# Attention's value loads put two groups ahead into the weights' raw buffers, and zero matmuls in the gaps before the gather

## The chip, the core and the metric

The kernel runs on one core of a Trainium2 chip, as one program in one launch. The metric is the device time of that launch in microseconds (us). Before the change its median is 881.94 us over three runs, 879.71 to 887.55.

## The reference

Three layers run one after the other, all in float32:

- attention over q, k, v of shape 4 x 12 x 448 x 64, with a sigmoid in place of the softmax: `sigmoid(q k^T / 8 - log 448) v`. Its output is the matrix x of 1792 tokens by 768;
- a mixture of 8 experts in which every expert takes exactly 224 tokens. The 1792 x 8 logits `x @ w_gate` are walked from the largest down; a pair (token, expert) is taken where the token is still free and the expert not yet full. Each expert then computes `relu(x @ w1[e]) @ w2[e]` on its tokens;
- a dense layer on the result: `h = x @ w_in`, `g = s * relu(h)^2 + b`, `g @ w_out`.

## The kernel before, in words

The order of the work is written out by hand: each engine runs its instructions in the order in which the Python code names them, and semaphores do the rest. All loads of the first stages are issued by one queue, SP, in order; a load whose buffer is not free holds back everything behind it. SP's transfers carry eight completion counters in turn, so a transfer also waits until the one eight places ahead has landed.

**Attention** runs over 12 groups `q` (three to each of the 4 batches). A group is two pairs `2q` and `2q+1` of two heads. Its values are one tile `vt` (128 x 7 x 128: three blocks of 128 keys for each pair, and in the middle the last 64 keys of both), loaded by `load_v` into two buffers. A pair's q and k are one tile `rqk`, loaded by `load_qk` in two transfers into five buffers. Each group has two halves, and in each half the code names:

- `split_qk`, on DVE: `rqk` of a pair of group q+2 is cut into a high part `wh` (L282) and a rest `wl` (L283);
- `values(q, half)`, on PE: the sigmoid weights times `vt` (L334, and L328 for the last 64 keys);
- every third group, for the batch before: `gate` and `gate_turn` (L354, L366);
- `scores(q+1, ...)`, on PE: three matmul terms of `wh` and `wl` for each block of keys (L310), each followed by a sigmoid on ACT;
- `convert`, on DVE (three times in group 4, else once or twice a group): w_in and w_out come as 64-bit floats and are made 32-bit in five DVE steps (four for later ones), from `craw` (768 KB a load, `cv_in`) to `co`, which goes back to memory as `nw` (`cv_out`). A `craw` load waits for the third of those steps (L155).

At the start of group q SP is given `load_qk` for the pairs 2q+5 and 2q+6 and `load_v` for group q+1. In the last two groups the first four experts' weights are loaded too (`w_dma`, five buffers `raw` of 128 x 768).

**The auction** then finds the assignment in eight steps (`auction`), a chain of small operations that hands from DVE to PE to DVE. In its gaps PE transposes x to rows (L508), ACT copies them out and SP stores them to `xs`. `keep_clock` (L418) multiplies zeros into a bank of PSUM that nobody reads.

**The places**: `settle` and `places` turn the choice into a list of row numbers `idx`: a running count (L612 to L618), 16 one-hot tiles `oh` on DVE (L626), 32 matmuls with them on PE (L634), two sums on DVE (L638). POOL then gathers the first expert's rows `xr` (L648). While that runs, PE is given `WARM[1]` zero matmuls; all engines then read a flag that decides the branch into more auction steps. PE goes on with 12 transposes of `xr` (L748) and the first expert's matmuls (L757 with `wh`, L758 with `wl`). From here to the end PE has work nearly all the time.

Of the kernel before, what the change touches and what calls it, by code (L numbers as in the profile page):

```python
# [8 lines left out]
F32 = mybir.dt.float32  # L9
# [10 lines left out]
B, H, S, D = 4, 12, 448, 64  # L20
# [4 lines left out]
CP = 112  # L25
NC = S // CP
NCH = NT // CP
# [9 lines left out]
STEPS = 8  # L37
MORE = (3, 8)
AHEAD = (2, 3, 4, 5, 6)
WARM = (7, 10, 2, 3)  # L40
ROWS = (3, 3, 3, 2, 2, 2, 2, 2)
SYNC = 0
SIGNS = 2
# [3 lines left out]
NQ = B * NP // 2  # L47
# [15 lines left out]


@with_exitstack
def tile_kernel(ctx, tc, qT, kT, v, wg, w1, w2, wi, wo, s2, b2, cst, out):
    nc = tc.nc
    V, A, G, T = nc.vector, nc.scalar, nc.gpsimd, nc.tensor

# [50 lines left out]
    cgp = early.enter_context(tc.tile_pool(name="cgp", bufs=1))  # L120

    att = ExitStack()
    qk = att.enter_context(tc.tile_pool(name="qk", bufs=5))
    vp = att.enter_context(tc.tile_pool(name="vp", bufs=2))
    at = att.enter_context(tc.tile_pool(name="at", bufs=2))
    ps_s = att.enter_context(tc.tile_pool(name="ps_s", bufs=3, space=PSUM))
# [9 lines left out]
    def cv_in():  # L136
        if todo:
            i = todo.pop(0)
            src, k, n = wide[i]
            craw[i] = cgp.tile([128, 768, 2], I32, name="craw", bufs=3)  # L140
            nc.sync.dma_start(craw[i].rearrange("p a b -> p (a b)"), src[n].bitcast(I32).rearrange("p k c -> p (k c)"))
            coming.append(i)
# [117 lines left out]
        nu["use"] += 1  # L260
        return splits.pop(i)

    raw_qk, two_qk, vt, attn, pvs, plg, lgs, pts = {}, {}, {}, {}, {}, {}, {}, {}
    pairs = [(b, p) for b in range(B) for p in range(NP)]

    def load_v(q):
        vt[q] = vp.tile([128, 7, 128], F32, name="vt", bufs=2)
        nc.sync.dma_start(vt[q], v[q // 3, q % 3])

    def load_qk(i):  # L270
        b, p = pairs[i]
        r = qk.tile([128, 2, S], F32, name="rqk")
        nc.sync.dma_start(r[:, 1], kT[b, p])
        nc.sync.dma_start(r[:, 0], qT[b, p])
        raw_qk[i] = r
# [42 lines left out]
                    two_qk.pop(n)  # L318

    def values(q, block):  # L320
        v = vt[q]
        pvs[q, block] = pv = ps_v.tile([128, 512], F32, name="pv")
        if block:
            a = attn.pop((q, 3))
            for n in range(2):
                rows = slice(n * 64, n * 64 + 64)
                for j in range(2):
                    T.matmul(pvs[q, n][j * 64:(j + 1) * 64, :S], v[rows, 3, j * D:(j + 1) * D], a[rows, j],  # L328
                             start=(n == 1), stop=(n == 0), skip_group_check=True)
            done(q, 0)  # L330
        for c in range(3):
            a = attn.pop((q, 4 * block + c))
            for j in range(2):
                T.matmul(pv[j * 64:(j + 1) * 64, :S], v[:, 4 * block + c, j * D:(j + 1) * D], a[:, j],  # L334
                         start=(block == 0 and c == 0), stop=(block == 1 and c == 2), skip_group_check=True)
        if block:
            done(q, 1)
# [75 lines left out]
    zero = ep.tile([128, 512], BF16, name="zero")  # L413
    V.memset(zero, 0.0)

    def keep_clock(n, p):
        for _ in range(n):
            T.matmul(p, zero[:, :CP], zero, start=True, stop=True)  # L418

    keep_clock(WARM[0], small_psum()[:CP])  # L420
    warm = ep.tile([1, 1], F32, name="warm")
# [8 lines left out]
    load_qk(2)  # L430
    load_qk(3)
    cv_in()
    cv_in()
    cv_in()
    scores(0, range(7))
    load_qk(4)
    nc.sync.dma_start(sb2[:, 0:1], s2.partition_broadcast(128))
    nc.sync.dma_start(sb2[:, 1:2], b2.partition_broadcast(128))
    G.memset(on, 1.0)
# [12 lines left out]
    for q in range(NQ):  # L452
        b, t = divmod(q, 3)
        closing = b == B - 1
        for n in (2 * q + 5, 2 * q + 6):
            if n < 2 * NQ:
                load_qk(n)
        if q + 1 < NQ:
            load_v(q + 1)
        for half in range(2):  # L460
            if q + 2 < NQ:
                split_qk(2 * q + 4 + half)
            values(q, half)
            if t == 0 and b:
                if half:
                    gate_turn(b - 1, True)
                    prefs(b - 1)
                else:
                    gate(b - 1, 0, NP, NP)
                    gate_copy(b - 1)  # L470
            if closing and 1 <= 2 * t + half <= 4 and 2 * t + half != 2:
                bracket((2 * t + half) // 2)
            if closing and t == 2 and not half:
                gate(b, 0, NP - 2, NP - 2)
                gate_copy(b)
            scores(q + 1, range(4, 7) if half else range(4))
            n = 2 * (NQ - q) - half
            if 2 < n <= 6:
                w_dma()
            for _ in range({4: 1, 3: 1, 2: 2}.get(n, 0)):  # L480
                w_high()
            for _ in range(CONV[2 * q + half]):
                convert()
            while nu["low"] < nu["high"]:
                w_low()
# [48 lines left out]
        T.matmul(pv, rival, aw, start=True, stop=True)  # L534
        return pv

    def settle(pv):
        V.scalar_tensor_tensor(ch, aw, 0.0, pv, op0=ALU.mult, op1=ALU.is_gt, accum_out=cnt0)

    def auction(n, fill):  # L540
        for it in range(n):
            if fill and it == 0:
                pv = choose(dv[0], pw)
                V.tensor_copy(WT, pw)
            else:
                pv = choose(dv[0])
            pc = ps_1.tile([128, LEVELS + 2], F32, name="pb")
            T.matmul(pc, two, off, start=True, stop=False)
            got = rows_in(ROWS[it] if fill else 2)
            if fill:  # L550
                keep_clock(WARM[3] if it == 0 else 2 * (it > 2), ps_r.tile([CP, 512], F32, name="pi"))
            if it or not fill:
                G.tensor_scalar(dv[0][:, 1:], dv[1][:, 1:], cut, least, op0=ALU.mult, op1=ALU.max)
                G.tensor_scalar(th, kvec, dv[0][:, 1:2], dv[0][:, 0:1], op0=ALU.mult, op1=ALU.add)
            V.scalar_tensor_tensor(LM, pv, -BIG, LT, op0=ALU.mult, op1=ALU.min)

            def sign(k, t):
                with nc.allow_low_precision(reason="whole numbers up to 112"):
                    A.activation(junk[3 + k % 3], LM, AF.Sign, bias=t, scale=-1.0, accum_out=cnt[:, k:k + 1])

            sign(0, dv[0][:, 0:1])
            for k in range(LEVELS):
                tk = th[:, k:k + 1]
                if k >= LEVELS - SIGNS:
                    sign(k + 2, tk)
                else:
                    V.scalar_tensor_tensor(junk[k % 3], LM, 0.0, tk.to_broadcast([128, CP]), op0=ALU.add, op1=ALU.is_ge,
                                           accum_out=cnt[:, k + 2:k + 3])
            rows_out(got)
            ns = LEVELS + 2 - SIGNS  # L570
            T.matmul(pc[:, ns:], nege, cnt[:, ns:], start=False, stop=False)
            T.matmul(pc[:, :ns], samee, cnt[:, :ns], start=False, stop=True)
            if fill:
                if it == 0:
                    rows(1)
                elif it > 2:
                    keep_clock(1, ps_r.tile([CP, 512], F32, name="pi"))
                if it in AHEAD:
                    w_dma()
            dv.reverse()  # L580
            V.scalar_tensor_tensor(jd, pc[:, 1:], FULL, dv[1], op0=ALU.is_ge, op1=ALU.mult,
                                   accum_out=dv[0][:, 0:1])
            V.scalar_tensor_tensor(jf, pc, FULL, fvec, op0=ALU.is_ge, op1=ALU.mult, accum_out=cut)
        settle(choose(dv[0]))

    flag = rp.tile([1, 1], I32, name="flag")

# [19 lines left out]
    oh = rp.tile([CP, NCH, CAP], BF16, name="oh")  # L607
    Pf = P.rearrange("p c e -> p (c e)")

    def places(rest=lambda: None):  # L610
        pp = ps_1.tile([CP, 128], F32, name="pa")
        T.matmul(pp, ch, identb, start=True, stop=True)  # L612
        V.tensor_copy(cw, cnt0.to_broadcast([128, CP]))
# [1 line left out]
        pof = po.rearrange("p c e -> p (c e)")  # L615
        T.matmul(pof, cw, prev, start=True, stop=False)
        V.tensor_copy(Pf, pp)
        T.matmul(pof, tri[:CP, :CP], Pf, start=False, stop=True)  # L618
        pc = claims()
        G.tensor_mul(R[:, :, 0, :], P, ct[:CP, C_CIDX:C_CIDX + 128].rearrange("p (c e) -> p c e", e=E))  # L620
# [11 lines left out]
        for c in range(NCH):  # L632
            for h, n in enumerate(HT):
                T.matmul(pis[h].rearrange("p a e -> p (a e)"), oh[:, c, h * 128:h * 128 + n],  # L634
                         R[:, c].rearrange("p a e -> p (a e)"), start=(c == 0), stop=(c == NCH - 1))
        for h, n in enumerate(HT):
            with nc.allow_low_precision(reason="whole numbers below 1792"):
                V.reduce_sum(idx[:n, h], pis[h].rearrange("p a e -> p e a"), axis=AX.X)  # L638
# [15 lines left out]
        rows(len(turns))  # L654
        keep_clock(3, ps_r.tile([CP, 512], F32, name="pi"))

    places(last_rows)
    keep_clock(WARM[1], ps_t.tile([CP, NC, 128], F32, name="px").rearrange("p c n -> p (c n)"))
    def greedy():
        mk = rp.tile([128, CP], F32, name="mk")  # L660
# [625 lines left out]
def _layout(np, i):  # L1286
    c = np.ascontiguousarray

    def heads(a):
# [7 lines left out]
    return {  # L1297
        "qT": c(heads(i["q"]).transpose(0, 1, 2, 4, 3).reshape(B, NP, 128, S)),
        "kT": c(heads(i["k"]).transpose(0, 1, 2, 4, 3).reshape(B, NP, 128, S)),
        "v": c(np.concatenate([main[:, :, 0], tail, main[:, :, 1]], axis=3)),  # L1300
        "wg": c(i["moe_w_gate"].reshape(KD, 128, E).transpose(1, 0, 2)),
        "w1": c(i["moe_w1"].reshape(E, KD, 128, KF, 128).transpose(0, 3, 2, 1, 4)),
        "w2": c(i["moe_w2"].reshape(E, KF, 128, KD, 128).transpose(0, 3, 1, 2, 4).reshape(E, KF, KD, 128, 128)
# [25 lines left out]
```

## Time and profile before

| what | value |
|---|---|
| median of three runs | 881.94 us (879.71 to 887.55) |
| the profiled execution | 882.63 us |
| its span, first to last instruction | 880.8 us |
| PE busy | 856.3 us, 97% |
| DVE busy | 642.6 us, 73% |
| ACT busy | 509.4 us, 58% |
| chain that ended last | PE 89%, DMA 5%, DVE 2%, ACT 1% |
| mean granted TensorE clock | 0.987 of full |

The span runs from the first to the last instruction; the profiled execution's time has 1.8 us around it. A row of a timeline gives start, duration, engine, line, operation, output and inputs, how often, and in brackets how long the engine sat idle before it and what ended that. The chain of waits is followed back from the last instruction, so its rows are pieces of the path that set the end. [...]

### The profile page before, as it was taken

To read this page: it belongs to the slowest core of one execution; us is meant where nothing else is said; L and a number is where in the kernel's file an instruction comes from. 1 tells how busy PE (TensorE), PEld (TensorE's weight loads), DVE (VectorE), ACT (ScalarE), POOL (GpSimd) and SP (SyncE) were. 2 spreads that over 40 slices of the span, in tenths; PEclk is the share of its full clock that TensorE was granted. 3 is DMA by queue.
4 is the path that set the end of the run, shared out by engine and by line. 5 is a ranking of instruction groups with operands and counts; after the bars stand their busy time and mean duration, and the time that the engine had idled before them with its cause. 6 is when DMAs were issued, how large, how long until landed. Compare 5 with 4: busy or idle time off the path is not lost.

```text
span 880.8 us, 14238 instructions
## 1 busy us (share of the span) xinstructions
PE 856.3 (97%) x5188; PEld 746.9 (85%) x5188; DVE 642.6 (73%) x1113; ACT 509.4 (58%) x887; POOL 85.0 (10%) x146
## 2 busy tenths in 40 slices
PE   9898999879999999999999999999999999999997
PEld 4444454649999999999999999999999999999997
DVE  2978786756778776779768776877887766857681
ACT  6466567745755566753565546767666555645440
POOL 1000000123000000000155422000000000000003
PEclk9899999999999999999999999999999999999999
DMA  8889796666668786658899987676653433332313
GB/s 297 303 295 353 268 381 231 187 205 223 208 200 287 244 291 208 209 187 304 280 335 319 301 238 247 194 234 185 225 180 98 128 107 116 112 106 91 101 37 132
DMA packets 76778, 190.40 MB, mean 216 GB/s; under 512 B 9120, under 2 KB 31136, under 8 KB 76448
## 3 DMA queue, kind: packets, MB, share of 16 engines
q1 hardware_dynamic: 68800, 164.28, 55.7%
q0 software_dynamic: 7904, 25.17, 10.1%
q8 instruction: 42, 0.69, 0.3%
q14 instruction: 32, 0.26, 0.1%
HBM read 161.11 MB, written 42.47 MB: 231 GB/s over the span
## 4 chain that ended last, share of the span: by engine, by line
PE 89%; DMA 5%; DVE 2%; ACT 1%; issue 1%; SPq 1%; POOL 0%; POOLq 0%; DVEq 0%; ACTq 0%
PE acc L757 16%; PE acc L758 8%; PE acc L1072 7%; PE acc L1071 7%; PE acc L1069 7%; PE pv L334 6%; PE psc L310 5%; PE acc L915 4%; PE acc L914 4%; PE acc L916 4%; PE acc L1178 4%; PE acc L1180 4%; PE acc L1179 4%; DMA vt<-in_v_dram 3%; PE acc L783 1%; PE acc L784 1%
## 5 line engine op out<-in xcount | busy, mean ns | idle before, releaser
L244 ACT CAST wh<-raw 128x768 fp32r<-128x768 f32 (+1 forms) x248 | 201.5, 823 | 91.0 <-issue 66.5
L254 DVE TENSOR_TENSOR wl<-raw,wh 128x768 fp32r<-128x768 f32 (+1 forms) x248 | 229.5, 937 | 21.3 <-PE acc L1071 11.3
L757 PE MATMUL acc<-u,wh 128*128 128x448 f32 x384 | 120.8, 374 | 0.0
L758 PE MATMUL acc<-u,wl 128*128 128x224 f32 x384 | 101.6, 265 | 0.2 <-DVE wl L254 0.2
L757 PE MATMUL acc<-x,wh 128*128 128x448 f32 x288 | 95.0, 384 | 0.6 <-issue 0.6
L313 ACT ACTIVATE attn<-psc,nls 128x896 f32<-128x896 f32 x84 | 78.0, 1009 | 29.9 <-PE psc L310 29.9
L758 PE MATMUL acc<-x,wl 128*128 128x224 f32 x288 | 76.9, 267 | 0.0
L757 PEld LDWEIGHTS acc<-u,wh 128*128 128x128 f32 x384 | 72.0, 188 | 5.3
L758 PEld LDWEIGHTS acc<-u,wl 128*128 128x128 f32 x384 | 73.3, 191 | 0.4 <-DVE wl L254 0.4
L334 PE MATMUL pv<-attn,vt 128*64 128x448 f32 x288 | 62.9, 574 | 8.5 <-DMA vt<-in_v_dram 8.5
L914 PE MATMUL acc<-y,wh 128*128 128x448 f32 x192 | 70.8, 369 | 0.0
L915 PE MATMUL acc<-y,wh 128*128 128x448 f32 x192 | 70.2, 366 | 0.0
L916 PE MATMUL acc<-y,wl 128*128 128x448 f32 x192 | 70.1, 365 | 0.0
L762 ACT COPY tmp<-acc 128x224 f32<-128x224 f32 x96 | 33.0, 343 | 48.9 <-PE acc L758 48.6
L757 PEld LDWEIGHTS acc<-x,wh 128*128 128x128 f32 x288 | 55.0, 191 | 4.8 <-issue 0.9
L334 PEld LDWEIGHTS pv<-attn,vt 128*64 128x64 f32 x288 | 19.7, 141 | 44.5 <-issue 41.6
L1069 PE MATMUL acc<-wh,as 128*128 128x384 f32 x168 | 56.1, 334 | 0.0
L1071 PE MATMUL acc<-wl,as 128*128 128x384 f32 x168 | 56.1, 334 | 0.0
L1072 PE MATMUL acc<-wh,as 128*128 128x384 f32 x168 | 56.1, 334 | 0.0
L758 PEld LDWEIGHTS acc<-x,wl 128*128 128x128 f32 x288 | 55.8, 194 | 0.3 <-DVE wl L254 0.3
L763 DVE TENSOR_TENSOR tmp<-acc,tmp 128x224 f32<-128x224 f32 x78 | 30.1, 385 | 27.9 <-ACT tmp L762 27.5
L648 POOL DMA_INDIRECT xr<-xs,idx x16 | 16.8, 1050 | 262.2 <-PE px L748 250.1
(338 smaller groups left out, 1974.2 us busy)
## 6 DMA issues: line engine op xcount, KB each, us to landing
raw<-in_w_dram SPq DMA_DIRECT2D x128, 384.0 KB, 3.8
raw<-nw SPq DMA_DIRECT2D x64, 384.0 KB, 3.7
craw<-in_wi_dram SPq DMA_DIRECT2D x16, 768.0 KB, 6.6
raw<-mx SPq DMA_DIRECT2D x32, 384.0 KB, 5.0
nw<-co SPq DMA_DIRECT2D x24, 384.0 KB, 7.3
craw<-in_wo_dram SPq DMA_DIRECT2D x8, 768.0 KB, 6.1
ra<-in_wo_dram SPq DMA_DIRECT2D x8, 768.0 KB, 5.3
hs<-nw POOLq DMA_DIRECT2D x16, 384.0 KB, 9.7
```

Source lines behind the costliest of these rows:

```text
L244: A.copy(h, r)
L254: eng.tensor_sub(lo, r, h.bitcast(F32))
L313: A.activation(attn[q, r], p[:, :, :S], AF.Sigmoid, bias=nls, scale=1.0 / math.sqrt(D))
L334: T.matmul(pv[j * 64:(j + 1) * 64, :S], v[:, 4 * block + c, j * D:(j + 1) * D], a[:, j], start=(block == 0 and c == 0), stop=(block == 1 a ...
L757: T.matmul(p[:, :2 * CAP], wh, src[:, k].rearrange("p a s -> p (a s)"), start=(k == 0), stop=False)
L758: T.matmul(p[:, :CAP], wl, src[:, k, 0], start=False, stop=(k == n - 1))
L914: T.matmul(p, wh, src[:, k, 0], start=first, stop=False)
L915: T.matmul(p, wh, src[:, k, 1], start=False, stop=False)
L916: T.matmul(p, wl, src[:, k, 0], start=False, stop=last)
L1069: T.matmul(acc, hi, wh[:, cols], start=(opens[j] and u == 0 and c == 0), stop=False, skip_group_check=True)
L1071: T.matmul(acc, hi, wl[:, cols], start=False, stop=False, skip_group_check=True)
L1072: T.matmul(acc, lo, wh[:, cols], start=False, stop=(u == 3 and c == 1), skip_group_check=True)
```

## The change

Three things change.

- The values of a group are one tile of 128 x 6 x 128 in the pool `raw` (five buffers, which the experts' weights use later). The last 64 keys of three groups of a batch come in one tile `vr` of 128 x 3 x 128, in two buffers. `load_v` is called for group q+2 in place of q+1, and for groups 0 and 1 before the loop.
- `rqk` has six buffers in place of five, and a group's start loads the pairs 2q+6 and 2q+7. The load of pair 5 joins that of pair 4 ahead of `scores(0)`.
- Zero matmuls: in the last auction step one more ahead of its counts and two more behind them, one in `settle`, one in `places` ahead of L618, one of 256 columns behind each pair of L634 from the fourth to the fifteenth, and 14 in place of 10 ahead of the branch.

```diff
-WARM = (7, 10, 2, 3)
+WARM = (7, 14, 2, 3)
...
-    qk = att.enter_context(tc.tile_pool(name="qk", bufs=5))
+    qk = att.enter_context(tc.tile_pool(name="qk", bufs=6))
...
     def load_v(q):
-        vt[q] = vp.tile([128, 7, 128], F32, name="vt", bufs=2)
+        vt[q] = wraw.tile([128, 6, 128], F32, name="raw")
         nc.sync.dma_start(vt[q], v[q // 3, q % 3])
+        if q % 3 == 0:
+            vr[q // 3] = vp.tile([128, 3, 128], F32, name="vr")
+            nc.sync.dma_start(vr[q // 3], vrest[q // 3])
...
     def values(q, block):
-        v = vt[q]
+        v, rest = vt[q], vr[q // 3][:, q % 3]
...
-                    T.matmul(pvs[q, n][j * 64:(j + 1) * 64, :S], v[rows, 3, j * D:(j + 1) * D], a[rows, j],
+                    T.matmul(pvs[q, n][j * 64:(j + 1) * 64, :S], rest[rows, j * D:(j + 1) * D], a[rows, j],
...
-                T.matmul(pv[j * 64:(j + 1) * 64, :S], v[:, 4 * block + c, j * D:(j + 1) * D], a[:, j],
+                T.matmul(pv[j * 64:(j + 1) * 64, :S], v[:, 3 * block + c, j * D:(j + 1) * D], a[:, j],
...
-    def keep_clock(n, p):
+    def keep_clock(n, p, w=512):
         for _ in range(n):
-            T.matmul(p, zero[:, :CP], zero, start=True, stop=True)
+            T.matmul(p[:, :w], zero[:, :CP], zero[:, :w], start=True, stop=True)
...
     cv_in()
+    load_v(1)
     cv_in()
     cv_in()
+    load_qk(4)
+    load_qk(5)
     scores(0, range(7))
-    load_qk(4)
...
-        for n in (2 * q + 5, 2 * q + 6):
+        for n in (2 * q + 6, 2 * q + 7):
             if n < 2 * NQ:
                 load_qk(n)
-        if q + 1 < NQ:
-            load_v(q + 1)
+        if q + 2 < NQ:
+            load_v(q + 2)
...
-    def settle(pv):
+    def settle(pv, fill=False):
+        if fill:
+            keep_clock(1, ps_r.tile([CP, 512], F32, name="pi"))
...
-                keep_clock(WARM[3] if it == 0 else 2 * (it > 2), ps_r.tile([CP, 512], F32, name="pi"))
+                keep_clock(WARM[3] if it == 0 else 2 * (it > 2) + (it == n - 1), ps_r.tile([CP, 512], F32, name="pi"))
...
-                    keep_clock(1, ps_r.tile([CP, 512], F32, name="pi"))
+                    keep_clock(3 if it == n - 1 else 1, ps_r.tile([CP, 512], F32, name="pi"))
...
-    def places(rest=lambda: None):
+    def places(rest=lambda: None, fill=False):
...
+        if fill:
+            junk_p = ps_t.tile([CP, NC, 128], F32, name="px").rearrange("p c n -> p (c n)")
+            keep_clock(1, junk_p)
         T.matmul(pof, tri[:CP, :CP], Pf, start=False, stop=True)
...
+            if fill and 2 < c < NCH - 1:
+                keep_clock(1, junk_p, 256)
```

The front of SP's queue, from the table of constants on, before the change (`ct` is the constants, `wgs` the gate's weights, `sb2` two scalars; the numbers tell tiles apart):

```order
L426 DMA ct_84<-in_cst_dram 128x1269
L268 DMA vt_228<-in_v_dram 128x896
...
L141 DMA craw_238<-in_wi_dram 128x1536
L141 DMA craw_240<-in_wi_dram 128x1536
L141 DMA craw_242<-in_wi_dram 128x1536
L273 DMA rqk_281<-in_kT_dram 128x448
L274 DMA rqk_281<-in_qT_dram 128x448
...
L273 DMA rqk_309<-in_kT_dram 128x448
L274 DMA rqk_309<-in_qT_dram 128x448
L268 DMA vt_312<-in_v_dram 128x896
L141 DMA craw_366<-in_wi_dram 128x1536
```

The same place now:

```order
L429 DMA ct_84<-in_cst_dram 128x1269
L268 DMA raw_228<-in_v_dram 128x768
L271 DMA vr_230<-in_vrest_dram 128x384
...
L141 DMA craw_240<-in_wi_dram 128x1536
L268 DMA raw_242<-in_v_dram 128x768
L141 DMA craw_244<-in_wi_dram 128x1536
L141 DMA craw_246<-in_wi_dram 128x1536
L276 DMA rqk_248<-in_kT_dram 128x448
L277 DMA rqk_248<-in_qT_dram 128x448
L276 DMA rqk_251<-in_kT_dram 128x448
L277 DMA rqk_251<-in_qT_dram 128x448
```

The values of group 1 (`vt_312`, now `raw_242`) went from behind the pairs 5 and 6 to a place behind the first `craw`; pair 4 (`rqk_281`, now `rqk_248`) has one value load and one tile of last keys more in front of it.

PE's queue in `places`, from the flag's count on, before the change (`oh` is a one-hot tile, `pi` the sums):

```order
L596 MATMUL pb<-on,ok 1x1
...
L634 LDWEIGHTS oh
L634 MATMUL pi<-R,oh 128x16
L634 LDWEIGHTS oh
L634 MATMUL pi<-R,oh 96x16
L634 LDWEIGHTS oh
L634 MATMUL pi<-R,oh 128x16
```

The same place now, from the fourth pair on:

```order
L644 LDWEIGHTS oh
L644 MATMUL pi<-R,oh 128x16
L644 LDWEIGHTS oh
L644 MATMUL pi<-R,oh 96x16
L421 LDWEIGHTS zero
L421 MATMUL px<-zero 112x256
L644 LDWEIGHTS oh
L644 MATMUL pi<-R,oh 128x16
```

Twelve zero matmuls of 256 columns stand between the pairs; before there was nothing between them.

## Rows read from the trace of the kernel before

**Rows 1.** The chain that ended last; columns: start us, us, what.
```profile
19.19 6.93 DMA vt<-in_v_dram
26.26 4.75 PE pv L334 x12
...
52.94 1.63 PE psc L354 x12
...
80.95 7.20 DMA vt<-in_v_dram
88.29 3.67 PE pv L334 x12
91.96 2.08 PE psc L354 x12
...
113.81 2.41 PE pv L334 x12
...
124.44 2.41 PE pv L334 x12
...
187.73 0.60 PE pi L634 x12
```

**Rows 2.** Timeline of PE, attention: the value blocks that waited for their load.
```profile
26.26 4.75 PE L334 MATMUL pv<-attn,vt 128*64 128x448 f32 x12 [4.64 <-DMA vt<-in_v_dram]
...
50.47 2.06 PE L334 MATMUL pv<-attn,vt 128*64 128x448 f32 x9 [0.38 <-DMA vt<-in_v_dram]
...
88.29 3.67 PE L334 MATMUL pv<-attn,vt 128*64 128x448 f32 x12 [3.31 <-DMA vt<-in_v_dram]
```

**Rows 3.** Windows of 10 us: PE busy (count), granted clock, DMA share, GB/s.
```profile
20.00:30.00 10.00, 5.36 (x26) 0.73 0.76 255
...
80.00:90.00 10.00, 6.69 (x46) 0.97 1.00 347
```

**Rows 4.** Timeline of SP: the issue of group 5's values.
```profile
67.16 0.39 SPq L268 DMA_DIRECT2D vt<-in_v_dram  x1
```

**Rows 5.** The tile vt: its 12 loads from issue to landing.
```profile
DMA to landing us min/median/max: 5.3/6.8/8.3
```

**Rows 6.** Timeline of DVE: the splits of pair 4 and pair 5.
```profile
19.83 0.63 DVE L282 CAST wh<-rqk 128x896 fp32r<-128x896 f32 x1 [4.64 <-DMA rqk<-in_qT_dram]
20.49 1.09 DVE L283 TENSOR_TENSOR wl<-rqk,wh 128x896 fp32r<-128x896 f32 x1
...
24.89 0.62 DVE L282 CAST wh<-rqk 128x896 fp32r<-128x896 f32 x1
```

**Rows 7.** Timeline of all engines at the auction's end: PE's two waits for DVE.
```profile
184.64 0.21 PE L534 MATMUL pa<-aw,cb 128*128 128x112 bf16 x1 [0.37 <-DVE aw L532]
...
185.23 0.26 PE L612 MATMUL pa<-cb,ch 128*112 128x128 bf16 x1 [0.38 <-DVE ch L538]
```

**Rows 8.** Timeline of DVE, the last ten one-hot tiles.
```profile
188.04 1.94 DVE L626 TENSOR_SCALAR oh<-slot,pos 112x224 bf16<-112x224 bf16 x10
```

**Rows 9.** Timeline of PE, from the places to the first expert.
```profile
190.12 2.35 PE L418 MATMUL px<-zero 128*112 128x512 bf16 x10
195.29 2.47 PE L748 MATMUL acc<-ident,xr 128*128 128x128 f32 x12 [2.82 <-DMA xr<-xs,idx]
...
198.38 0.71 PE L757 MATMUL acc<-x,wh 128*128 128x448 f32 x1 [0.61 <-issue]
...
202.01 0.41 PE L757 MATMUL acc<-x,wh 128*128 128x448 f32 x1
```

**Rows 10.** Windows of 1 us: busy of PE, PEld, DVE, ACT, POOL; clock, DMA share, GB/s.
```profile
159.00:160.00 1.00, 1.00 (x7) 1.00 (x6) 0.13 (x1) 0.00 (x0) 0.00 (x0) 0.50 0.00 0
...
161.00:162.00 1.00, 0.92 (x6) 0.39 (x4) 0.52 (x3) 1.00 (x3) 0.00 (x0) 0.95 0.05 14
...
194.00:195.00 1.00, 0.00 (x0) 0.00 (x0) 0.00 (x0) 0.00 (x0) 0.00 (x0) 1.00 0.75 205
...
197.00:198.00 1.00, 0.77 (x5) 0.47 (x3) 1.00 (x3) 0.92 (x3) 0.92 (x1) 0.50 0.00 0
```

More of the change, by code (lines that the diff above doesn't have):

```diff
@@ L65, in tile_kernel @@
 @with_exitstack
-def tile_kernel(ctx, tc, qT, kT, v, wg, w1, w2, wi, wo, s2, b2, cst, out):
+def tile_kernel(ctx, tc, qT, kT, v, vrest, wg, w1, w2, wi, wo, s2, b2, cst, out):
     nc = tc.nc
@@ L261, in w_get @@
         return splits.pop(i)
-    raw_qk, two_qk, vt, attn, pvs, plg, lgs, pts = {}, {}, {}, {}, {}, {}, {}, {}
+    raw_qk, two_qk, vt, vr, attn, pvs, plg, lgs, pts = {}, {}, {}, {}, {}, {}, {}, {}, {}
     pairs = [(b, p) for b in range(B) for p in range(NP)]
     def load_v(q):
-        vt[q] = vp.tile([128, 7, 128], F32, name="vt", bufs=2)
+        vt[q] = wraw.tile([128, 6, 128], F32, name="raw")
         nc.sync.dma_start(vt[q], v[q // 3, q % 3])
+        if q % 3 == 0:
+            vr[q // 3] = vp.tile([128, 3, 128], F32, name="vr")
+            nc.sync.dma_start(vr[q // 3], vrest[q // 3])
     def load_qk(i):
@@ L583, in auction @@
             V.scalar_tensor_tensor(jf, pc, FULL, fvec, op0=ALU.is_ge, op1=ALU.mult, accum_out=cut)
-        settle(choose(dv[0]))
+        settle(choose(dv[0]), fill)
     flag = rp.tile([1, 1], I32, name="flag")
@@ L655, in last_rows @@
         keep_clock(3, ps_r.tile([CP, 512], F32, name="pi"))
-    places(last_rows)
+    places(last_rows, True)
     keep_clock(WARM[1], ps_t.tile([CP, NC, 128], F32, name="px").rearrange("p c n -> p (c n)"))
@@ L1299, in _layout @@
         "kT": c(heads(i["k"]).transpose(0, 1, 2, 4, 3).reshape(B, NP, 128, S)),
-        "v": c(np.concatenate([main[:, :, 0], tail, main[:, :, 1]], axis=3)),
+        "v": c(np.concatenate([main[:, :, 0], main[:, :, 1]], axis=3)),
+        "vrest": c(tail.transpose(0, 2, 3, 1, 4).reshape(B, 128, 3, 128)),
         "wg": c(i["moe_w_gate"].reshape(KD, 128, E).transpose(1, 0, 2)),
```

## The prediction

> **What bounds the kernel now.** I read the chain of waits first, for pieces that are not PE's work. In attention it changes over to a DMA at two loads of the values, and each time the block of value matmuls behind it takes longer than elsewhere [rows 1]. PE's timeline gives the pauses: 4.64 us ahead of group 1, 3.31 ahead of group 6, 0.38 ahead of group 3 [rows 2]. The windows show the granted clock below full in both places [rows 3]. So attention is bound by PE, broken by value loads. A third break is the gather: PE sits 2.82 us behind its last zero matmul, and the clock, 1.00 before, is 0.50 for the first transposes and matmuls [rows 9, 10]. From there PE is busy to the end, so what is saved ahead stays saved.
>
> **Attention, step by step.** A value block takes 2.41 us at full clock [rows 1].
>
> - Group 1: 4.64 us of waiting, and the block takes 4.75 at the low clock, 2.34 too much: 6.98.
> - Group 3: 0.38.
> - Group 6: 3.31; its block takes 3.67, 1.26 too much, and the gate behind it 2.08 where an earlier one takes 1.63 [rows 1]: 0.45. Together 5.02.
>
> The three make 12.38 us. What does the change do to them? Group 1's values are now issued behind the first `craw`, ahead of two more `craw` and two pairs, so what used to be ahead of them in the queue is behind. Group 6's values are issued a whole group earlier, where group 5's were: at 67.2 us instead of 81.0 [rows 1, 4]. With the slowest landing, 8.3 us [rows 5], they are there at 75.5. Without the first two losses PE would want them at 85.0 - 7.4 = 77.6 (85.0 is 88.29 less 3.31). So all three waits go.
>
> What is late next? The splits on DVE, which feed the scores. Group 2's scores need pair 4, whose split starts at 19.83, after a 4.64 us wait for the load, and takes 1.75 (from 19.83 to 20.49 + 1.09) [rows 6]. One value load (384 KB) and 128 KB more for the first last-keys tile now land ahead of it: 512 KB at the 347 GB/s of a slice in which the DMA engines are full [rows 3] is 1.5 us. DVE is ready at 19.83 + 1.5 + 1.75 = 23.1. PE used to reach group 1 at 21.6 (26.26 less 4.64) and does its value block in 2.41, so it asks for pair 4 at 24.0. The slack is 0.9 us. After that the two run side by side: a half of DVE's work takes 5.06 us (19.83 to 24.89), a group 10.1; a group of PE's takes 10.63 (113.81 to 124.44) [rows 1, 6], more with a gate. PE stays the slower one, except in group 4 with its third conversion. The pairs' loads themselves come a buffer earlier than before, so DVE's own waits shrink. I take the splits as covered; if that cover is gone, the price is in the third case.
>
> A small cost: the 128 KB come ahead of the pairs 2 and 3 too, whose splits PE already waits for in group 0: 0.4 us by the same rate. If those splits keep pace it is 0. I take 0.3.
>
> Four more transfers (`vr`), and one SP issue each, lie beside other work: the issue in row group 4 takes 0.39 us. At the end of attention the third and fourth weight load may wait for a `raw` buffer that PE still reads values from; SP then holds back only stores of converted weights, which nobody in attention reads. I cost it at 0.
>
> Attention: **12.1 us** gained.
>
> **The zero matmuls.** One costs 0.22 us (ten from 190.12 take 2.35 with the last one's end) [rows 9]. The two more behind the last step's counts and the one in `settle` fall into PE's waits for DVE of 0.37 and 0.38 us [rows 7]; the one in `places` and the one ahead of the counts likewise stand before instructions that wait for another engine. Bounds 0 to 5 x 0.22 = 1.1; I take 0, since PE has waits on both sides of them.
>
> The twelve between the one-hot pairs: DVE makes a tile in 0.19 us (1.94 for ten) [rows 8], and PE did twelve matmuls, six pairs, in 0.60 where the tiles were there [rows 1], 0.10 a pair. Half of 0.22 more makes 0.21, so PE falls behind by 0.02 a tile and by what it was late at the start. Bounds: 0, if DVE still sets the pace, and 12 x 0.11 = 1.3, if nothing overlaps. I take 0.35, near the lower, since 0.21 is close to 0.19. All behind it, the gather too, moves by that.
>
> The four more ahead of the branch lie inside the gather's time: PE's 2.82 us wait becomes 2.82 - 4 x 0.22 = 1.9. They cost nothing, since they end before the rows land. What do they bring? If the clock stays up, six pairs of L757 and L758 that take 3.63 us (198.38 to 202.01) take half of that at twice the clock, 1.8 less [rows 9]. The transposes, 2.47 us for twelve, would halve; but ACT and DVE have to cut their results, so of 1.2 us I count 0.5, between 0.3 (the first three alone) and 1.2. Together 2.3. If the clock falls all the same, it is 0. The rows hold a pause of 2.82 us after which the clock fell, and two of 0.4 a few us earlier, after which it was still 1.00 at 194 [rows 7, 9, 10]; 1.9 lies between. I take the gain, since the pause is cut by a third and the stretch before it is fuller; the other end is the second case.
>
> **Sum**, against the profiled execution's 882.63: 12.1 and 2.3 off, 0.35 on, makes 868.6. That execution is 0.7 above the median of 881.94, so the forecast is **868**.
>
> **The cases.** About 1%, 8.8 us, is what a measurement of this kernel can tell from no change: faster begins below 873.1, slower above 890.8.
>
> 1. As summed: 868. Chance 0.46.
> 2. The waits go, but the clock falls after the gather: 870.2. Chance 0.25. For it: 1.9 us is still a pause, followed by transposes only. Against: the pause that is known to cost was half as long again. [...]
> 3. The wait moves from the values to the splits: DVE gets pair 4 or 5 late. For it: the slack is 0.9 us, and DVE has waited 4.64 us for that very load [rows 6]. With another such delay PE waits 4.64 - 0.9 = 3.7, and if the clock falls, 2.3 more as in group 1: of the gain 6 are lost, 874. Against: what was put ahead is 1.5 us of transfer, and pairs 4 and 5 now stand ahead of the small loads that followed them. Chance 0.15.
> 4. The value loads still come late, because SP stands behind DVE's conversions whatever the order says: 882.3. Against: the issue of a group earlier is in the trace at 67.2 us. Chance 0.08.
> 5. Slower: the transfers are the bound, not their order. Then 384 + 448 KB brought forward (a value load and a pair) push every later load by 2.4 us at 347 GB/s, DVE waits for `craw` and pairs in place of PE for values, none of the 12.4 goes, and with one more fall of the clock (6.98 - 4.64 = 2.3) and the 0.35 the time is 882.6 + 2.4 + 2.3 + 0.35 - 0.7 = 887; a second such fall makes 889, a third 891. It decides from the point where the 16 DMA engines have no idle time left in the first 90 us. Against: from 20 to 30 they were 0.76 busy while PE waited; for: 1.00 from 80 to 90 [rows 3]. Chance 0.06.
>
> Cases 1 and 2, 0.71, are faster by over 1%; of case 3, which lies at the bound, I count 0.05 there and 0.10 within 1%; case 4 is within, and case 5 mostly within by its price, but a delay that repeats makes it slower, so I split it 0.02 and 0.04. That makes 0.76, 0.20 and 0.04. The range, 865.5 to 876, begins where the two small costs are 0 and the transposes give their 1.2 (866.7), with 1 us for the spread of the runs shown, whose lowest is 2.2 under the median; it ends above the third case with 2 us more of waiting. Cases 4 and 5, 0.14, are left out.
>
> **What would show it.** PE's value blocks are free of waits for a DMA, and all twelve take 2.4 us; the clock is 1.00 from 20 to 100 us. DVE's first split starts before 21.5. The 32 one-hot matmuls with their zeros take about 2.75 us where they took 2.4 (187.73 in the chain to 190.12). PE's pause before the transposes is near 1.9, and the clock in it and behind it is 1.00. I am wrong if PE waits for `wl` or `wh` in groups 1 to 6, if the clock falls after the gather, or if DMA engines are full and values still land late.

## The result, and the profile after

| what | before | after |
|---|---|---|
| median | 882.49 us (six runs, 879.71 to 887.55) | 871.14 us (six runs, 869.92 to 872.18) |
| ratio after to before, 95% interval | | 0.987 (0.984 to 0.990) |
| the profiled execution, its span | 882.63, 880.8 us | 871.05, 869.2 us |
| mean granted TensorE clock | 0.987 | 0.997 |

The kernel is faster by 11.3 us. A second measurement, beside experiments 5, 10 and 11, gave 871.75 us and a ratio of 0.990 (0.988 to 0.992). The forecast was 868, the range 865.5 to 876. One run of experiment 6 took 1399.58 us at a mean granted clock of 0.556 and is left out of that experiment's numbers.

**Attention.** The chain of waits of the changed kernel (start us, us, what), at the places that [rows 1] showed before: the first blocks of groups 1, 3 and 6, the last with the gate behind it, and the gather.

```profile
22.32 2.41 PE pv L337 x12
...
43.58 2.41 PE pv L337 x12
...
78.03 2.41 PE pv L337 x12
80.43 1.63 PE psc L357 x12
...
177.69 4.42 DMA xr<-xs,idx
```

No value load is left in it, every block takes 2.4 us, the gate 1.63. The windows of 10 us that stood in [rows 3] now read (length; PE busy and count, PEld, DVE, ACT, POOL; clock, DMA share, GB/s):

```profile
20.00:30.00 10.00, 10.00 (x74) 5.42 (x74) 8.43 (x12) 7.46 (x9) 0.00 (x0) 1.00 0.86 290
80.00:90.00 10.00, 10.00 (x78) 5.30 (x76) 9.71 (x14) 5.39 (x8) 0.00 (x0) 1.00 1.01 378
```

PE is busy throughout at full clock, also where the DMA engines have no idle time left. The two loads in question, on SP's timeline, are issued at 10.21 (group 1) and 64.42 (group 6):

```profile
10.21 0.33 SPq L268 DMA_DIRECT2D raw<-in_v_dram  x1
...
64.42 0.42 SPq L268 DMA_DIRECT2D raw<-in_v_dram  x1
```

The split of pair 4 came later, as feared, but not too late. DVE's timeline, to be held against [rows 6]:

```profile
21.43 0.63 DVE L285 CAST wh<-rqk 128x896 fp32r<-128x896 f32 x1 [5.57 <-DMA rqk<-in_qT_dram]
22.09 1.09 DVE L286 TENSOR_TENSOR wl<-rqk,wh 128x896 fp32r<-128x896 f32 x1
```

It ends at 23.18, and PE reaches the scores that need it at 24.66.

**From the places to the first expert.** PE's timeline, which answers to [rows 9], preceded by the row of the scores just mentioned:

```profile
24.66 0.47 PE L313 MATMUL psc<-wh 64*128 64x448 f32 x2
...
177.08 3.21 PE L421 MATMUL px<-zero 128*112 128x512 bf16 x14
182.71 1.35 PE L760 MATMUL acc<-ident,xr 128*128 128x128 f32 x12 [2.42 <-DMA xr<-xs,idx]
185.38 0.67 PE L769 MATMUL acc<-x,wh 128*128 128x448 f32 x1 [1.33 <-DVE x L763]
...
188.78 0.30 PE L770 MATMUL acc<-x,wl 128*128 128x224 f32 x1
```

And the windows of 1 us there (columns as above), beside [rows 10]:

```profile
183.00:184.00 1.00, 1.00 (x12) 0.86 (x9) 0.10 (x1) 0.61 (x2) 0.17 (x1) 1.00 0.00 0
184.00:185.00 1.00, 0.05 (x1) 0.00 (x0) 1.00 (x3) 0.85 (x3) 0.79 (x1) 1.00 0.00 0
185.00:186.00 1.00, 0.61 (x2) 0.61 (x3) 0.65 (x2) 0.00 (x0) 0.90 (x1) 0.72 0.47 92
186.00:187.00 1.00, 1.00 (x5) 0.94 (x4) 0.00 (x0) 0.00 (x0) 0.01 (x1) 0.50 0.82 305
```

The pause is shorter, 2.42 where it was 2.82, and the clock stays 1.00 through it and through the transposes, which take 1.35 where they took 2.47. Then PE waits 1.33 us for DVE to cut their results, and the clock falls at the end of that wait: it is 0.72 over the slice from 185, 0.50 over the next two and 0.58 over the one from 188, some 3.4 us at 0.50 in all, in which the first six pairs run, as they ran at 0.50 before.

**Where the 11.6 us of the span went,** cut at instructions that both traces have:

| stretch | before | after | gained |
|---|---|---|---|
| start to the logits of the last batch (L372, now L375) | 156.06 | 144.10 | 11.96 |
| to the first one-hot matmul | 31.61 | 30.19 | 1.42 |
| one-hot matmuls, first to last | 2.41 | 2.74 | -0.33 |
| to the end of `idx` | 0.43 | 0.44 | -0.01 |
| gather, end of `idx` to the first transpose | 4.78 | 5.24 | -0.46 |
| to the first expert matmul | 3.09 | 2.67 | 0.42 |
| from there to the end | 682.4 | 683.8 | -1.4 |

Rows two, five and seven are not what the forecast counted on; the experiments say what they are.

### The profile page after: what moved, and what is told of

Its sections match the earlier page's. It is cut to its first block, busy times and chain, and to the rows that moved or that the text cites. A ratio compares the mean times of both kernels' runs of the same rounds, so it can differ in the third digit from the quotient of the medians.

```text
span 869.2 us, 14278 instructions
## 1 busy us (share of the span) xinstructions
PE 853.7 (98%) x5209; PEld 745.1 (86%) x5209; DVE 642.5 (74%) x1113; ACT 509.2 (59%) x887; POOL 84.5 (10%) x146
## 4 chain that ended last, share of the span: by engine, by line
PE 92%; DVE 2%; ACT 2%; DMA 1%; issue 1%; SPq 1%; POOL 0%; POOLq 0%; ACTq 0%; DVEq 0%
PE acc L769 16%; PE acc L770 8%; PE acc L1081 7%; PE acc L1084 7%; PE acc L1083 7%; PE psc L313 6%; PE pv L337 6%; PE acc L926 5%; PE acc L927 4%; PE acc L928 4%; PE acc L1190 4%; PE acc L1192 4%; PE acc L1191 4%; PE acc L795 1%; PE acc L796 1%; PE acc L797 1%
## 5 line engine op out<-in xcount | busy, mean ns | idle before, releaser
L337 PE MATMUL pv<-attn,raw 128*64 128x448 f32 x288 | 59.4, 548 | 0.0
L337 PEld LDWEIGHTS pv<-attn,raw 128*64 128x64 f32 x288 | 18.5, 136 | 34.8 <-issue 32.0
```

The lines of the kernel that those rows point to most:

```text
L337: T.matmul(pv[j * 64:(j + 1) * 64, :S], v[:, 3 * block + c, j * D:(j + 1) * D], a[:, j], start=(block == 0 and c == 0), stop=(block == 1 a ...
```

## Experiments

Each kernel was timed in five rounds; the medians of before beside them were 881.69, 880.87 and 880.79 us.

**1. The attention part alone.** All new zero matmuls out:

```diff
-WARM = (7, 14, 2, 3)
+WARM = (7, 10, 2, 3)
...
-    places(last_rows, True)
+    places(last_rows)
```

(and so in `settle` and the last auction step).

> The change's attention part alone: values in the raw buffers two groups ahead, six buffers for q and k, and no zero matmul beyond those of the kernel before. Theory A (all of the gain is the value loads' waits and the clock that fell behind them): 870.8 us, between 869.8 and 871.9; attention's end 12 us earlier than before, the 32 one-hot matmuls in 2.4 us as before, PE's pause ahead of the transposes back at 2.8, the clock 0.50 for the first transposes. Rival Z (the zero matmuls carry some microseconds of the gain by holding the clock): 873 or more.

Measured: 871.92 us (870.11 to 873.13), ratio 0.989 (0.987 to 0.992). Within its spread that is the changed kernel's time. PE before the first expert, and two windows (columns as above):

```profile
177.66 3.77 PE L421 MATMUL px<-zero 128*112 128x512 bf16 x10
183.42 1.97 PE L760 MATMUL acc<-ident,xr 128*128 128x128 f32 x12 [1.99 <-DMA xr<-xs,idx]
```

```profile
174.00:175.00 1.00, 1.00 (x4) 0.24 (x2) 0.96 (x7) 0.58 (x1) 0.00 (x0) 0.50 0.81 241
...
184.00:185.00 1.00, 1.00 (x8) 0.99 (x7) 0.39 (x1) 0.90 (x3) 0.30 (x1) 0.50 0.00 0
```

The clock is low in the places and again from 184. With the clock at 0.50 ahead of them (the slice from 176) and 0.72 over the slice from 180, the ten zeros took 3.77 us, so the pause was 1.99 and not the 2.8 expected. That the missing zeros let the clock fall in the places is not shown: the kernel before has none of them either, and its clock was 1.00 there (186 to 190 us). On the median none of this is to be seen.

**2. The zero matmuls alone,** on the kernel before (the diff's lines from `keep_clock` on, and `WARM`).

> The change's zero matmuls alone, attention as before. Theory A: 882 to 883.5, no change that can be measured: the twelve between the one-hot matmuls cost 0.3, the four ahead of the branch give the transposes 0.4 to 0.5 back. The value blocks of groups 1 and 6 wait for their loads as before. Rival Z: 880.5 or less, with the clock at 1.00 behind the gather.

Measured: 880.95 us (878.93 to 884.28), ratio 1.000 (0.998 to 1.002): nothing. PE's timeline still has both waits:

```profile
24.87 4.01 PE L334 MATMUL pv<-attn,vt 128*64 128x448 f32 x12 [3.01 <-DMA vt<-in_v_dram]
...
86.37 3.98 PE L334 MATMUL pv<-attn,vt 128*64 128x448 f32 x12 [2.39 <-DMA vt<-in_v_dram]
```

Behind its gather the profile is like the changed kernel's: a pause of 2.64 us, transposes in 1.37, a wait of 1.33 for DVE.

**3. Only the order of the value loads** (`v_early`): the pairs as before.

```diff
-    qk = att.enter_context(tc.tile_pool(name="qk", bufs=6))
+    qk = att.enter_context(tc.tile_pool(name="qk", bufs=5))
...
-    load_qk(4)
-    load_qk(5)
     scores(0, range(7))
+    load_qk(4)
...
-        for n in (2 * q + 6, 2 * q + 7):
+        for n in (2 * q + 5, 2 * q + 6):
```

> The changed kernel, but rqk has five buffers and the pairs are loaded when and where they were before; only the values' loads are moved. Theory (the order of the value loads is the whole gain): no value block waits for a load, attention's last gate starts near 144, and the time is 871 to 872. Rival (pairs and values share one queue, so the earlier pairs are what makes room): the waits come back on the splits; DVE's split of pair 4 starts later than 21.4, PE waits for wh or wl in group 1 or 2, and the time is 874 or more. Second rival (the sixth buffer is the cause, the values' place is not): 880 to 882.

Measured: 871.04 us (868.63 to 872.96), ratio 0.990 (0.988 to 0.991). The split of pair 4, on DVE's timeline:

```profile
21.49 0.63 DVE L285 CAST wh<-rqk 128x896 fp32r<-128x896 f32 x1 [6.16 <-DMA rqk<-in_qT_dram]
```

It starts within 0.06 us of the changed kernel's, PE waits for nothing in attention from 12 us on, and the last batch's logits start at 144.06. The sixth buffer and the earlier pairs bring nothing that can be measured. This profile also bears on the zeros: the gather took 4.81 us, so the pause was 1.99, near the forecast 1.9, and the clock fell all the same, in the transposes. PE's timeline, and a window:

```profile
183.51 2.38 PE L759 MATMUL acc<-ident,xr 128*128 128x128 f32 x12 [1.99 <-DMA xr<-xs,idx]
```

```profile
184.00:185.00 1.00, 0.97 (x6) 0.57 (x5) 0.28 (x1) 0.79 (x2) 0.09 (x1) 0.50 0.02 6
```

**4. Everything but that order** (`v_late`).

```diff
-    load_v(1)
...
-        if q + 2 < NQ:
-            load_v(q + 2)
+        if q + 1 < NQ:
+            load_v(q + 1)
```

> The changed kernel, but load_v is called for group q+1 in the loop as before, and not for group 1 ahead of it; the tiles in the raw pool, the six rqk buffers and the earlier pairs stay. Theory: the value blocks of groups 1 and 6 wait 4.6 and 3.3 us again and the clock falls there, so the time is 881 to 883. Rival (the sixth buffer or the smaller value tile is the cause): 871 to 873. A middle value, 875 to 877, would say that one of the two waits was removed by the pairs.

Measured: 881.17 us (877.08 to 884.20), ratio 1.000 (0.998 to 1.002). PE's timeline has the waits of [rows 2] again:

```profile
27.09 4.75 PE L337 MATMUL pv<-attn,raw 128*64 128x448 f32 x12 [4.46 <-DMA raw<-in_v_dram]
...
88.09 2.48 PE L337 MATMUL pv<-attn,raw 128*64 128x448 f32 x12 [3.02 <-DMA raw<-in_v_dram]
```

Both ends are closed: without the order all the rest gives nothing, and with it the gain stays when the sixth buffer (experiment 3) or the zeros (experiment 1) are taken out. One thing differs from [rows 2]: behind the wait of 3.02 us the block took 2.48, and the clock was 1.00 there (80 to 90 us).

**5. The values of group 1 alone late** (`v1_late`).

```diff
-    load_v(1)
...
+        if q == 0:
+            load_v(1)
         if q + 2 < NQ:
             load_v(q + 2)
```

> The changed kernel, but the values of group 1 alone are loaded in the loop, behind the pairs 6 and 7, where they were before. Theory (groups 1 and 6 are lost apart from each other, 6.98 and 5.02 us): group 1 waits some 4.6 us with the clock low behind it, every later value block waits for nothing, and the time is 871 + 7 = 878. Rival (a delay at group 1 gives the later loads time, and one lost there need not be lost at group 6): no more to see at group 6, and 876 or less, because attention's DVE, which runs ahead in the pause, shortens later waits. Second rival (the early load of group 1 only moves the wait on): 871 to 873.

Measured: 876.33 us (874.31 to 879.37), ratio 0.996 (0.994 to 0.997), beside 871.75 for the changed kernel: 4.6 us for group 1, not 7. PE's timeline, and the window:

```profile
25.29 2.48 PE L337 MATMUL pv<-attn,raw 128*64 128x448 f32 x12 [3.51 <-DMA raw<-in_v_dram]
```

```profile
20.00:30.00 10.00, 6.49 (x52) 4.05 (x52) 9.79 (x15) 4.47 (x6) 0.00 (x0) 1.00 0.87 287
```

The profiled execution, the fastest of the nine at 874.31, has a wait of 3.51 us and a clock of 1.00 in every slice of attention that was read (up to 95 us and from 140 on); its logits of the last batch start at 147.05, 2.7 behind the 144.35 of the changed kernel's second profile. Group 6 waits for nothing (80.95, without a wait); since its load is early here, that alone doesn't tell the theory from the first rival, and the time lies nearer to the rival's 876. But the rival's mechanism is not in the trace: PE was ready for group 1 at 21.78 here (25.29 - 3.51) and at 22.56 in that second profile, and 3.51 less these 0.78 is 2.73, so no later wait gave any of it back. What was wrong in the theory is the low clock: a wait isn't always followed by it.

**6. Ten zeros ahead of the branch in place of 14** (`warm10`): `WARM = (7, 10, 2, 3)`, the other zeros kept.

> The changed kernel with 10 in place of 14 zero matmuls ahead of the branch, the other zeros kept. Theory A: 871.0 to 872.0: the pause ahead of the transposes is 3.3 us, the clock falls in it, twelve transposes take 2.4 instead of 1.35 and the first expert matmul comes 0.4 later. Rival B (fourteen overshoot: PE's branch code behind them makes the transposes late): the transposes start 0.3 to 0.4 sooner behind the row numbers than the 5.5 us of the changed kernel, and the time is 870.5 to 871.

Measured: 871.76 us (871.35 to 872.70, five runs), ratio 0.990 (0.987 to 0.993). PE's timeline, and a window:

```profile
177.97 2.35 PE L421 MATMUL px<-zero 128*112 128x512 bf16 x10
183.72 1.93 PE L760 MATMUL acc<-ident,xr 128*128 128x128 f32 x12 [3.40 <-DMA xr<-xs,idx]
```

```profile
184.00:185.00 1.00, 1.00 (x10) 1.00 (x8) 0.10 (x1) 0.61 (x2) 0.04 (x1) 0.65 0.00 0
```

With four zeros fewer the pause is 3.40 and the clock falls in the transposes, not behind them. The gather takes 5.36 us from `idx`, no less than the 5.24 with 14, so nothing here speaks for the 14 holding the branch up; one profile of each can't rule it out, since the gather's time varies (4.78 to 6.25 us over the profiles).

**7. Matmuls in the wait behind the transposes** (`hold`), with the 14 zeros ahead:

```diff
+    pf = ps_x.tile([128, 512], F32, name="px")
+    for _ in range(5):
+        T.matmul(pf[:, :128], ident, ident, start=True, stop=True)
     gather(1)
```

> The changed kernel with five matmuls of the identity by itself (128 columns, into a bank nobody reads) between the first expert's transposes and its first matmul, where PE waits 1.33 us for DVE. Theory W (it is that wait which takes the clock down at 185.4): the clock stays at 1.00, six pairs of the first expert's matmuls take 1.9 us instead of 3.5, and the time is 869.4, 1.7 less than the changed kernel. Rival P (the pause of 2.4 us ahead of the transposes takes it down, and only the reading comes later): the clock falls in the same place and the time is 871 as without them.

Measured: 870.51 us (868.41 to 871.99), ratio 0.988 (0.985 to 0.991). In the profiled execution the gather took 5.75 us, the longest so far, and the pause became 2.93:

```profile
184.06 2.37 PE L760 MATMUL acc<-ident,xr 128*128 128x128 f32 x12 [2.93 <-DMA xr<-xs,idx]
186.23 1.96 PE L1247 MATMUL px<-ident 128*128 128x128 f32 x10
187.95 0.45 PE L769 MATMUL acc<-x,wh 128*128 128x448 f32 x1
```

```profile
184.00:185.00 1.00, 0.94 (x5) 0.97 (x6) 0.00 (x0) 0.01 (x1) 0.00 (x0) 0.59 0.00 0
```

The clock fell at the end of the pause; the five matmuls took 1.96 us, 1.31 in experiment 8 (each is two records), and put the first expert off to 3.89 us behind the first transpose. In this execution the second filling alone was not enough. In another it may have been: one of the six runs took 868.41 us at a mean clock of 0.999, which is what the profile of experiment 8 has, where the clock held. The other half, 20 zeros without the five matmuls, was not run.

**8. Both gaps** (`hold20`): `WARM = (7, 20, 2, 3)` and the five matmuls.

> The changed kernel with 20 zero matmuls ahead of the branch in place of 14, and five 128-column matmuls of ident with itself between the first expert's transposes and its first matmul. Theory A (the clock falls where PE has been idle for long: 2.4 us before the rows and 1.3 us before x): the pause before the transposes is 1.1 to 1.6 us, the clock stays 1.00 through pause, transposes and the first six pairs of the first expert, and the time is 1.3 to 1.8 us under the changed kernel's: 869.3 to 869.8. Rival (the clock falls about there whatever PE does): it is 0.50 for 3.4 us somewhere from 183 to 190, and the time is 870.5 to 871.5. Second rival (the zeros run into the gather's end and hold up the branch): the pause is 0.6, the transposes start later than 5.7 behind idx, and the time is 871 to 872.5.

Measured: 870.83 us (869.79 to 872.56), ratio 0.990 (0.988 to 0.991). The clock holds: it is 1.00 in every slice of 1 us from 182 to 200. PE's timeline:

```profile
177.55 4.50 PE L421 MATMUL px<-zero 128*112 128x512 bf16 x20
183.05 1.48 PE L760 MATMUL acc<-ident,xr 128*128 128x128 f32 x12 [1.00 <-DMA xr<-xs,idx]
184.37 1.31 PE L1247 MATMUL px<-ident 128*128 128x128 f32 x10
185.73 0.44 PE L769 MATMUL acc<-x,wh 128*128 128x448 f32 x1
```

From 185.73 to the end of the span (868.0) it is 682.3 us, 1.6 less than the changed kernel's 683.8 (869.2 - 185.38). Yet its median is only 0.3 under the changed kernel's 871.14; in the profiled execution the mixed layer (`layer_mixed`, L1190 to L1192) went at the slower of two paces, on which experiment 12 says more.

**9. Both gaps, and nothing between the one-hot matmuls** (`hold20_bare`):

```diff
-            if fill and 2 < c < NCH - 1:
-                keep_clock(1, junk_p, 256)
```

> As the run with 20 zeros and the five matmuls, but without the twelve zero matmuls of 256 columns between the one-hot matmuls. Theory (they cost 0.33 us and hold nothing, since PE is idle only after them): the 32 one-hot matmuls take 2.2 to 2.4 us in place of 2.74, the clock is as in the run with them, and the time is 0.3 us lower. Rival (they carry the clock through the places): the clock falls to 0.50 between 173 and 181 as in the run of the attention part alone, the 20 zeros take twice their time and end behind the rows' landing, and the time is 1 to 3 us higher.

Measured: 868.61 us (868.15 to 868.86), ratio 0.986 (0.985 to 0.988). PE's timeline, and a window in which the changed kernel was at the low clock:

```profile
177.99 4.50 PE L421 MATMUL px<-zero 128*112 128x512 bf16 x20
183.24 0.85 PE L758 MATMUL acc<-ident,xr 128*128 128x128 f32 x6 [0.74 <-DMA xr<-xs,idx]
...
185.93 0.45 PE L767 MATMUL acc<-x,wh 128*128 128x448 f32 x1
```

```profile
186.00:187.00 1.00, 1.00 (x9) 0.96 (x8) 0.18 (x1) 0.00 (x0) 0.54 (x1) 1.00 0.85 190
```

The one-hot matmuls take 2.41 us, as before the change, and the clock is 1.00 in the places without them (173 to 178 us).

**10. The same once more** (`hold20_bare_again`), with the two next.

> The run with 20 zeros ahead of the branch, five matmuls behind the transposes and nothing between the one-hot matmuls, once more, beside the changed kernel. Theory: about 1.8 us for the low clock stretch behind the gather and 0.3 us for the twelve zeros, so 2.1 us under the changed kernel: 868.6 to 869.3. Rival (the first measurement was chance): within 1 us of it, 870 to 872.

Measured: 868.93 us (868.10 to 870.00), ratio 0.986 (0.984 to 0.989). Here the gather took 6.25 us:

```profile
184.03 1.34 PE L758 MATMUL acc<-ident,xr 128*128 128x128 f32 x12 [2.13 <-DMA xr<-xs,idx]
185.21 1.31 PE L1245 MATMUL px<-ident 128*128 128x128 f32 x10
186.71 0.44 PE L767 MATMUL acc<-x,wh 128*128 128x448 f32 x1 [0.19 <-issue]
```

The pause was 2.13, and the clock held all the same, 1.00 in every slice from 182 to 189. The eight runs of this kernel go from 868.10 to 870.00, the eleven of the changed kernel from 869.92 to 873.30. It beats both kernels; it is 2.5 to 2.8 us under the changed one. Of that 1.6 is the clock behind the gather and 0.33 the twelve zeros; 0.6 to 0.9 stays unexplained.

**11. Without the twelve zeros, nothing else** (`bare14`).

> The changed kernel without the twelve zero matmuls of 256 columns; 14 ahead of the branch and no matmuls behind the transposes, as it has. Theory (the twelve cost 0.33 us, and what the 20 zeros and the five matmuls hold is the other 1.8): the clock falls behind the gather as in the changed kernel, and the time is 870.5 to 871. Rival (the twelve zeros themselves cost the 2 us, by heating the throttle or by delaying the gather): 868.5 to 869.3.

Measured: 870.29 us (868.73 to 871.74), ratio 0.988 (0.985 to 0.990). The one-hot matmuls take 2.41 us, and PE's wait for `x` is there again:

```profile
185.50 0.44 PE L767 MATMUL acc<-x,wh 128*128 128x448 f32 x1 [0.78 <-DVE x L761]
185.78 0.33 PE L768 MATMUL acc<-x,wl 128*128 128x224 f32 x1
185.91 0.61 PE L767 MATMUL acc<-x,wh 128*128 128x448 f32 x1
```

The third row takes 0.61, and the clock is 0.92 over the slice from 185 and 0.50 over the next: it fell there, as in the changed kernel. The rest up to `hold20_bare`, 1.4 us by the medians of one group, is the filling of both gaps. By the same medians the twelve zeros alone would be 1.5 us (871.75 less 870.29), far more than the 0.33 in the loop. The four runs spread over 3.0 us, so the times don't rule out a part of the rival's cost. The traces show no place for it: without the twelve, in experiments 9 to 11, the gather took 4.86, 6.25 and 5.07 us, in the nine profiles with them 4.81 to 5.75; and the clock in the places is 1.00 with them (the changed kernel, 170 to 178 us) and without.

**12. The changed kernel once more** (`after_again`), no edit.

> The changed kernel once more, unchanged, beside the three others of this group. Theory (whether a stretch of 448-column matmuls of the mixed layer goes at 207 or at 203 ns apart is set anew in each execution): the time is 870 to 872 again, and the profiled execution may have either pitch from 676 to 742. Rival (the pitch belongs to the kernel): 207 ns again in the same stretch.

Measured: 871.75 us (871.35 to 873.30). Its trace tells what changes from execution to execution. The mixed layer's 448-column matmuls, grouped by line from 678 to 740 us (busy us, mean ns), first here, then in the first profile of the changed kernel from 676 to 742:

```profile
L1192 PE MATMUL acc<-x,wl 128*128 128x448 f32 x30 | 11.0, 365 | 0.0
```

```profile
L1192 PE MATMUL acc<-x,wl 128*128 128x448 f32 x30 | 11.0, 368 | 0.0
```

From start to start they are 202.7 ns apart here and 206.7 there, for some 65 us on end: 1.3 us, for one and the same kernel. And behind attention the clock is low, as it was in the kernel before (0.50 from 158 to 161) and was not in the first profile (1.00 from 140 to 160):

```profile
147.00:148.00 1.00, 1.00 (x7) 0.99 (x6) 0.38 (x2) 0.00 (x0) 0.00 (x0) 0.50 0.00 0
148.00:149.00 1.00, 1.00 (x7) 1.00 (x6) 0.00 (x0) 0.43 (x2) 0.00 (x0) 0.50 0.00 0
```

That stretch costs 1.4 us: from the logits to the first one-hot matmul it is 31.63 us here, 30.19 there.

With these two sorted out, the time from the first expert matmul to the end, in five executions, falls into four values:

| clock behind the gather | mixed layer at 202.7 ns | at 206.7 ns |
|---|---|---|
| fell | 682.4 (before), 682.5 (`after_again`) | 683.8 (after) |
| held | 681.0 (`hold20_bare`) | 682.3 (`hold20`) |

Across it is 1.3 to 1.4 us, down 1.5 to 1.6, and the two add up. The other nine profiles fit: at the fast pace 681.0 where the clock was at 1.00 from the first expert matmul on and 682.4 to 683.2 where it was not, at the slow pace, with the clock fallen, 683.8 to 684.6. So row seven of the table of stretches is the mixed layer's pitch and no work of the change, row two is the stretch behind attention, and row five is the gather, which took between 4.78 and 6.25 us in the executions profiled.

## Why the prediction was right, and where it failed

- **The mechanism of attention was right.** The value loads' order is the cause (experiments 3 and 4), all three waits went, and nothing took their place (the one wait that PE has left there, 0.53 us for `wl` in group 0, was 0.39 before). The case of late splits (0.15) did not come: DVE had the pair cut at 23.18, where 23.1 was forecast, and PE asked at 24.66 (24.0). Nor did the case of full DMA engines (0.06): from 80 to 90 us they were full (1.01), and no block waited. The case that the loads would still be late (0.08) fell with SP's rows.
- **Its size** was right for the profiled pair, 11.96 of 12.1, but that is partly luck, and it was too large for the medians: `v_late` lies 9.4 to 10.0 us above the changed kernel. The term that was mis-sized is the 12.38. It was read from one execution, the worst of the three that were profiled with the value loads in the old order: 8.33 us are its waits and 4.05 the low clock behind them (2.34 of group 1's 6.98, 1.71 of group 6's 5.02). Experiment 2's profile has 7.0 of waits and 3.0 of low clock, experiment 4's 7.5 and 2.3. So their last batch's logits start at 154.03 and 154.07, not at 156.06; in the ten profiles with the new order they start at 143.22 to 144.62. Of the three profiles that have a wait at group 1 and were taken after the forecast, two show the low clock there (4.01 and 4.75 us for the block) and `v1_late` doesn't; at group 6 one does (3.98), one doesn't (2.48). Put back by itself, group 1 costs 4.6.
- **The start cost** was forecast at 0.3, and the profiles can't tell it. DVE's first split of pair 2 starts at 12.45 in the changed kernel and at 11.77 in the kernel before, 0.7 later; but over the ten profiles with the new order it starts anywhere from 11.38 to 13.04.
- **The twelve zeros** cost 0.33 us in the one-hot loop, forecast 0.35, and hold nothing that the profiles show: in experiments 9 to 11 the clock in the places is 1.00 without them. The five zeros ahead of them cost nothing, as taken: with the clock low behind attention in both, the stretch from the logits to the first one-hot matmul is 31.61 before and 31.63 in experiment 12.
- **The step that failed** is "I take the gain": that four more zeros keep the clock behind the gather. The pause was 2.42, not 1.9, since the gather took 5.24 us instead of 4.78. That did not decide it: here the clock was 1.00 in the pause and in the transposes, while in experiment 3 the pause was 1.99 and the clock fell in the transposes. What the sum had not seen is the next gap: transposes at full clock make DVE the late one, PE's wait of 0.61 becomes 1.33, and the clock falls at its end. Of the 2.3 us the transposes' part came in this profile (0.42 for 0.5; not in those of experiments 3 and 5, where they took 2.38 and 2.13), the 1.8 for the six pairs did not; experiments 8 to 10 show that it is there, at 1.6, with both gaps filled.
- **Which case it was.** The second, 870.2, and 871.14 was measured. Its ground, a pause that is still a pause with only transposes behind it, held. In the changed kernel the clock fell after 5.1 us (2.42, 1.35 and 1.33) that held nothing but transposes; in the kernel before it came back, from 0.50 to 0.95 over the slice from 161, at the end of 3 us of little but transposes (158 to 161, [rows 10]). What transposes do to the clock is not shown, since no run here puts other matmuls in their place.
- **Two prices and a bound.** The 882.3 and 887 of cases 4 and 5 leave out the 2.3 us of clock that the sum takes off, without saying why, and 866.7 less 1 is 865.7, not 865.5. Neither matters for the outcome.
- **What is left,** 0.9 us between that case and the measured median, is of the size of what changes from one execution to the next.

## What to carry to other kernels

Where several streams share one queue, look for the consumer that waits and move its load, and it alone, up by one round: here the order of the value loads was worth all of some 10 us, and a sixth buffer for the pairs nothing. The price of a wait was its length and, in some executions, a low clock behind it (a block of 4.01 us behind a wait of 3.01, of 2.48 behind one of 3.51): read that part from several executions. Filling a gap to hold the clock did not pay here while the next gap stood open (pause at 1.00, six pairs at 0.50); count every gap up to the point from which the engine is busy, at the lengths that they will have at full clock.

## What the runs showed of the hardware that was not expected

- The same 448-column matmuls of one kernel go at 202.7 or at 206.7 ns from start to start, for 60 to 70 us on end, and which it is differs between executions (`after_again` beside after). What sets it was not found.
- Waits of much the same length are followed by the low clock in one execution and not in another: 3.01 us in experiment 2 (the block took 4.01), 3.51 in experiment 5 (2.48). Ahead of the transposes it is the same: the clock fell in them behind a pause of 1.99 us (experiment 3), and was 1.00 through them behind one of 2.42 (the changed kernel).
- The gather of the same rows took 4.78 to 6.25 us from `idx` to the first transpose, over the 14 profiles.
